# A two-layer transformer kernel: the normalised rows of the dense parts turned by way of DRAM and DVE instead of TensorE

## The chip, the cores and the metric

The kernel runs on one core of one Trainium2 chip. The metric is the device time of one execution in microseconds, as the median of several runs. Five engines are named as the profile names them: PE (TensorE, with its weight loads as PEld), DVE (VectorE), ACT (ScalarE), POOL (GpSimd) and SP (SyncE). Each has a queue of its own that it works off in order. Transfers are done by 16 DMA engines; in this kernel SP's queue issues them.

## The reference

A stack of attention, dense, attention, dense, over S = 2048 rows of D = 576 columns, with the same weights both times. The attention is linear, with 32 heads of 18 columns, the dense part has F = 4608 hidden features:

```python
x = A_x
x = x + _A_ref(_layernorm(x, axis=-1), A_wqkv, A_w_phi, A_wo)
x = x + _B_ref(_layernorm(x, axis=-1), B_w1, B_b1, B_w2, B_b2)
x = x + _A_ref(_layernorm(x, axis=-1), A_wqkv, A_w_phi, A_wo)
x = x + _B_ref(_layernorm(x, axis=-1), B_w1, B_b1, B_w2, B_b2)

def _B_ref(x, w1, b1, w2, b2):
    h = jnp.einsum("bsd,df->bsf", x, w1) + b1
    h = jnp.where(h > 0, h, 0) ** 2
    return jnp.einsum("bsf,fd->bsd", h, w2) + b2
```

`_A_ref` projects to queries, keys and values, applies a learned map and two softmaxes per head to queries and keys, forms the linear attention through the sums over all rows of key times value, and projects back. All sums over the rows' keys must be there before any row of that layer's attention can leave. `_layernorm` takes mean and variance of each row and has no weights.

## The kernel before, in words

**Tiles.** The rows are cut into 4 blocks of TB = 512, a block into NT = 4 tiles of P = 128. The 576 columns are KC = 4 chunks of 128 and one of DT = 64. Every operand of a matmul is split into a high part (rounded to the matmul's format) and a low part (what the rounding left), and three products stand for one. An operand must lie with the summed dimension on the partitions, so rows that were normalised must be turned: from 128 rows x 576 columns to columns x rows.

**The norm** (`Norm`, L329-397) works on one block. For tile t: `stats` (L351 and L360 on DVE, the reciprocal root on POOL), `scale` (L371, L372 on DVE: subtract the mean, multiply), `turn` (L386: four transposes of 128x128 on PE into PSUM; L387: the high part copied out by ACT; L388: the low part by DVE). For half h, which is two tiles, `rest` does the same with the last 64 columns (L395, L396, L397).

**The dense part** (`g_mlp`) runs per block over f = 0 to 35, each 128 hidden features. `hidden(f)` is 14 matmuls (L824), `square(f)` the bias, relu (L829, ACT), square (L830, ACT) and the split (L833 cast and L834 subtraction, DVE), `second(f - 1)` the way back, 12 matmuls by rows (L849) and 3 by features (L841). PE's order is hidden(f), second(f - 1), hidden(f + 1), and so on. The PSUM bank of `hidden` has one buffer from f = 2 on, so relu(f) must have read it before hidden(f + 1) starts. The weights come from DRAM by SP, one tile of 640 KB (`m_..h`, L787) and one of 576 KB (`m_..s`, L799) per f.

**What lies between.** `g_mlp` is a generator that yields after each hidden and each second. `weave` takes one slot of a plan at each yield, and the plan holds the attention's work, spread over the slots: `Plan.put(turn, depth, call)` puts a call into slot 2 x turn + 1, within a slot the greater depth first. The emitted order is each engine's order. A block of the dense part carries the attention of the next block (`plan_attend`), and in layer 0 also the keys and values of layer 1 for the block that was finished before it (`plan_keys`). Layer 0 works through blocks 3, 2, 0, 1, and layer 1 through 1, 0, 3, 2.

**The norms that the change touches.** `plan_norm` (L696) places one norm's steps. It is called in `plan_attend` (six norms: a_2, a_0, a_1 in layer 0 and a_0, a_3, a_2 in layer 1, in the last third of the dense block before) and in `plan_keys` (three norms, in the first iterations of a dense block: n_3 in m_2, n_2 in m_0, n_0 in m_1). The norms of the opening, of the passage between the layers and of the last keys are placed by other code and stay as they are. After `scale`, `out.keep` (L691) adds b2 to a row tile of the attend norms and stores it (L694); `g_mlp` loads it again at its end (L911). In `plan_keys`, `spill` writes the turned rows to DRAM for the second layer's queries.

In the profile m_2 is the dense part of block 2, a_0n.. the attend norm of block 0, n_2.. the keys norm of block 2, k_2.. the keys that follow it.

Of the kernel before, what the change touches and what calls it, by code (L numbers as in the profile page):

```python
# [21 lines left out]
def layers_kernel(  # L22
# [18 lines left out]
    nc = tc.nc  # L41
    S, D = x_in.shape[1], x_in.shape[2]
# [280 lines left out]
    def xt_tiles(name):  # L323
        return {"h": sb.tile([P, NC, TB], F32R, tag="xh", name=f"{name}h"),
                "l": sb.tile([P, KC, TB], F32R, tag="xl", name=f"{name}l")}

    class Norm:
# [62 lines left out]
        def rest(self, h):  # L390
# [5 lines left out]
            nc.scalar.activation(xh[:DT, KC, rows], pt[:DT, : TB // 2], AF.Copy)  # L396
            nc.vector.tensor_sub(xh[DT:, KC, rows], pt[:DT, : TB // 2], xh[:DT, KC, rows].bitcast(F32))  # L397
# [7 lines left out]
    def spill(b, x, parts=range(4)):  # L405
        for i in parts:
            d, piece = xt_part(b, x, i)
            nc.sync.dma_start(d, piece)
# [284 lines left out]
            nc.vector.tensor_add(x, x, b2t)  # L693
            nc.sync.dma_start(xm[self.b][t], x)  # L694

    def plan_norm(plan, norm, x_of, stats, scales, turns, rests, late=()):  # L696
        for t in range(NT):
            plan.put(stats[t], 0, lambda t=t: norm.stats(t, x_of(t)))
            plan.put(scales[t], 1, norm.scale, t)
            plan.put(turns[t], -1 if t in late else 2, norm.turn, t)  # L700
        for h in range(2):
            plan.put(rests[h], 2, norm.rest, h)

# [34 lines left out]
    def plan_attend(plan, at, gap, layer, b, raws, dst, name, o, queries=None):  # L738

        out = Out(layer, b, [], name)  # L740
        out.pair, calls = o
        if queries:
            for t in range(NT):
                plan.put(at + gap * t, 0, queries, t)
            at += 1
        for n, call in enumerate(calls):
            plan.put(at + n, 9, call)
        at = plan_queries(plan, at, gap, layer, raws, [], out.ph, name) + 1
        for i in range(2 * NG):
            plan.put(at + i / 2, 0, out.turn, i)  # L750
            plan.put(at + (i + 1) / 2, 1, out.times, i)
        at += NG + 1
        for t in range(NT):
            plan.put(at + t - 1, 9, out.load, t)
        plan_norm(plan, Norm(dst, f"{name}n", out.keep), out.project, [at + t for t in range(NT)],
                  [at + 1, at + 2, at + 4, at + 5], [at + 4 + t for t in range(NT)], [at + 5, at + 7])


    def g_mlp(layer, b, x, after, name, fresh, apart, final):
# [584 lines left out]
    def plan_keys(plan, prev_rows, last, keep):  # L1344
# [1 line left out]
        pb, done = prev_rows  # L1346
        m = f"1_{pb}"
        xk, es, ks, vts = {}, {}, {}, {}
        plan_norm(plan, Norm(xk, f"n{m}"), lambda t: done[t], (0, 0, 1, 2), (1, 1, 2, 3), (2, 3, 4, 4.5), (3, 5), (3,))
        (vw, vcalls), (kw, kcalls) = asked("v", f"w{m}"), asked("k", f"w{m}", TAGS_C)  # L1350
        for n in range(4):
            plan.put(8 + n if last else 2 + n / 2, 9, vcalls[n])
            plan.put(n / 2, 9, kcalls[n])
        if not last:
            for n in range(4):
                plan.put(5 + n / 2, -1, lambda n=n: spill(pb, xk, [n]))

        def keys(t):
            ks[t] = make_raw(xk, t, kw, f"k{m}k")
# [50 lines left out]
```

## Time and profile before

| | |
|---|---|
| median of 3 runs | 2529.17 us (2528.23 to 2530.25) |
| profiled execution, its own time | 2530.61 us |
| its span in the trace | 2528.9 us, 37324 instructions |
| granted TensorE clock | 1.00 in every stage |
| DMA packets of SP's queue | 161118, 503.10 MB |
| read from and written to DRAM | 418.39 and 84.64 MB, 199 GB/s over the span |

The span runs from the first to the last instruction of the trace; the run's own time has a little around it. A row of a timeline gives the start and the duration in microseconds, the engine, the line, the operation with its output and inputs, the shapes, how many equal neighbours are merged (x), and in brackets how long the engine stood idle before and what ended that. A row of the groups gives the count, the busy time in microseconds and the mean in ns, then the idle time ahead of the group. The layer's and the tile's number are left out of the names, so a_0np stands for all tiles of that kind in both layers.

### The profile page before, as it was taken

What the parts mean: (1) busy time and instruction counts of PE and PEld (TensorE: products, weight loads), DVE (VectorE), ACT (ScalarE), POOL (GpSimd) and SP (SyncE); (2) the same over time, 40 slices, a digit from 0 to 9 for tenths busy, and PEclk for the clock granted to TensorE, in tenths of its full rate; (3) what the DMA queues carried; (4) which work ended last, traced back from release to release, by engine and by line L of the source; (5) the groups of instructions that cost most, each with busy time, mean ns of one, the idle gap of its engine ahead of it and who ended that gap; (6) DMA issues with size and microseconds to landing.
All of it is one profiled execution on the core that took longest, in us unless ns stands there. A gap on an engine that the chain in (4) does not pass through costs nothing.

```text
span 2528.9 us, 37324 instructions
## 1 busy us (share of the span) xinstructions
PE 2512.7 (99%) x15300; PEld 2215.4 (88%) x15300; DVE 1166.8 (46%) x1986; ACT 741.9 (29%) x1268; POOL 113.4 (4%) x275
## 2 busy tenths in 40 slices
PE   9999999999999999999999999999999999999999
PEld 8998888888888988888888988888888888888887
DVE  6887955434634446345113775332353326332112
ACT  5544443322222222223223332222222222222221
POOL 4302000000000000000000010000000000000000
PEclk9999999999999999999999999999999999999999
DMA  9514887867647576484665345457544665456565
GB/s 318 174 53 138 288 280 259 309 216 265 214 148 261 179 262 213 147 272 147 196 198 168 115 142 189 152 192 258 183 161 155 221 231 164 148 187 230 195 193 174
DMA packets 161288, 505.48 MB, mean 200 GB/s; under 512 B 21350, under 2 KB 49798, under 8 KB 161118
## 3 DMA queue, kind: packets, MB, share of 16 engines
q1 hardware_dynamic: 161118, 503.10, 59.8%
q8 instruction: 121, 1.98, 0.3%
q14 instruction: 49, 0.40, 0.0%
HBM read 418.39 MB, written 84.64 MB: 199 GB/s over the span
## 4 chain that ended last, share of the span: by engine, by line
PE 97%; DMA 1%; DVE 1%; ACT 0%; issue 0%; SPq 0%; DVEq 0%; ACTq 0%
PE m_1ph L824 9%; PE m_3ph L824 9%; PE m_0ph L824 9%; PE m_2ph L824 9%; PE m_1acc L849 7%; PE m_3acc L849 7%; PE m_2acc L849 7%; PE m_0acc L849 7%; PE m_1acc L841 2%; PE m_3acc L841 2%; PE m_2acc L841 2%; PE m_0acc L841 2%; PE a_2po L686 1%; PE a_0po L686 1%; PE kvp L527 1%; PE a_3po L686 1%
## 5 line engine op out<-in xcount | busy, mean ns | idle before, releaser
L824 PE MATMUL m_2ph<-a_2nh,m_2h 128*128 128x512 f32 x720 | 225.4, 395 | 2.1 <-DMA m_2h<-dw 2.1
L824 PE MATMUL m_0ph<-a_0nh,m_0h 128*128 128x512 f32 x720 | 226.3, 396 | 0.2 <-DMA m_0h<-dw 0.2
L849 PE MATMUL m_3acc<-m_3s,m_3hb 128*128 128x448 f32 x864 | 189.7, 367 | 0.3 <-DVE m_3hb L833 0.3
L849 PE MATMUL m_0acc<-m_0s,m_0hb 128*128 128x448 f32 x864 | 189.9, 368 | 0.0
L849 PE MATMUL m_1acc<-m_1s,m_1hb 128*128 128x448 f32 x864 | 189.4, 367 | 0.3 <-PE m_1ph L824 0.3
L849 PE MATMUL m_2acc<-m_2s,m_2hb 128*128 128x448 f32 x864 | 189.6, 367 | 0.0
L849 PEld LDWEIGHTS m_1acc<-m_1s,m_1hb 128*128 128x128 f32 x864 | 161.5, 188 | 18.2 <-PE m_1ph L824 0.5
L833 DVE CAST m_2hb<-m_2hr 128x512 fp32r<-128x512 f32 x72 | 30.8, 427 | 317.8 <-ACT m_2hr L830 317.4
L849 PEld LDWEIGHTS m_3acc<-m_3s,m_3hb 128*128 128x128 f32 x864 | 161.2, 188 | 17.8 <-PE m_3ph L824 0.5
L849 PEld LDWEIGHTS m_2acc<-m_2s,m_2hb 128*128 128x128 f32 x864 | 160.7, 188 | 16.1
L849 PEld LDWEIGHTS m_0acc<-m_0s,m_0hb 128*128 128x128 f32 x864 | 160.3, 188 | 15.6
L824 PEld LDWEIGHTS m_2ph<-a_2nh,m_2h 128*128 128x128 f32 x720 | 135.3, 188 | 32.8 <-issue 2.5
L824 PEld LDWEIGHTS m_0ph<-a_0nh,m_0h 128*128 128x128 f32 x720 | 135.3, 188 | 30.5 <-issue 0.6
L833 DVE CAST m_1hb<-m_1hr 128x512 fp32r<-128x512 f32 x72 | 30.7, 427 | 269.2 <-ACT m_1hr L830 269.2
L829 ACT ACTIVATE m_2hr<-m_2ph,b1t 128x512 f32<-128x512 f32 x72 | 49.6, 689 | 353.7 <-PE m_2ph L824 353.7
L833 DVE CAST m_0hb<-m_0hr 128x512 fp32r<-128x512 f32 x72 | 30.8, 427 | 260.8 <-ACT m_0hr L830 255.2
L829 ACT ACTIVATE m_0hr<-m_0ph,b1t 128x512 f32<-128x512 f32 x72 | 49.6, 689 | 334.3 <-PE m_0ph L824 334.3
L829 ACT ACTIVATE m_1hr<-m_1ph,b1t 128x512 f32<-128x512 f32 x72 | 49.6, 689 | 323.2 <-PE m_1ph L824 323.2
L829 ACT ACTIVATE m_3hr<-m_3ph,b1t 128x512 f32<-128x512 f32 x72 | 49.6, 689 | 240.3 <-PE m_3ph L824 240.3
L824 PE MATMUL m_3ph<-t0onh,m_3h 128*128 128x512 f32 (+1 forms) x380 | 113.3, 385 | 0.7 <-ACT t0onh L387 0.5
L833 DVE CAST m_3hb<-m_3hr 128x512 fp32r<-128x512 f32 x72 | 30.7, 426 | 180.5 <-ACT m_3hr L830 180.5
L824 PE MATMUL m_1ph<-t1onh,m_1h 128*128 128x512 f32 (+1 forms) x380 | 113.2, 385 | 0.6 <-ACT t1onh L387 0.5
(1934 smaller groups left out, 5618.8 us busy)
## 6 DMA issues: line engine op xcount, KB each, us to landing
m_2h<-dw SPq DMA_DIRECT2D x72, 640.0 KB
m_0h<-dw SPq DMA_DIRECT2D x72, 640.0 KB
m_1h<-dw SPq DMA_DIRECT2D x72, 640.0 KB
m_2s<-dw SPq DMA_DIRECT2D x72, 576.0 KB
m_0s<-dw SPq DMA_DIRECT2D x72, 576.0 KB
m_1s<-dw SPq DMA_DIRECT2D x72, 576.0 KB
dw<-m_3h SPq DMA_DIRECT2D x36, 640.0 KB
m_3h<-dw SPq DMA_DIRECT2D x36, 640.0 KB
```

The source lines that it names most:

```text
L527: nc.tensor.matmul(po[32 * q : 32 * q + 32, :, j], vt[:, h * VW : h * VW + 32], e[:, :, h * DH : (h + 1) * DH], start=not stay, stop=True, ...
L686: nc.tensor.matmul(pt[:, :HP], a, m[:w, g], start=(g == 0 and k == 0), stop=(g == NG - 1 and k == 2))
L824: nc.tensor.matmul(ph[:, cols], a, m, start=(k == 0), stop=(k == 3 * KC + 1))
L829: nc.scalar.activation(hr, ph, AF.Relu, bias=b1t[:, f : f + 1])
L833: nc.vector.tensor_copy(hh, hr)
L841: nc.tensor.matmul(acc[KC], a, m, start=(f == 0 and k == 0), stop=(f == NF - 1 and k == 2))
L849: nc.tensor.matmul(acc[t][:, :R], a[:, rows], m, start=(f == 0 and k == 0), stop=(f == NF - 1 and k == 2))
```

## The change

A class `StoredNorm` takes the place of `Norm` in `plan_attend` and `plan_keys`. Its `scale` writes the scaled rows into a tile whose 4 x 4 blocks of 32 columns are exchanged. `store` (two transfers) writes them to DRAM in that order, `fetch` (one transfer, and for every odd tile another for the last 64 columns) reads them back with every fourth row in a partition group, so that after it the element (row, column) has to move within 32 x 32 only. `turn` and `rest` then use DVE's transpose of 32 x 32 blocks (L438, L449), ACT copies the high part (L441, L452), DVE subtracts for the low part (L442, L453); the reordering left is in the access patterns of these three. All these transfers are issued by ACT. `store` stands half a turn, which is one slot, after `scale`; `fetch` has a time of its own. Both have depth -1, so they come last in their slot. For the keys norms stats and scales move forward, turns and rests half a turn back, and the spill one turn back; for the attend norms two scales move forward by a turn, and turns and rests stay. The 9 norms have 20 transposes each on PE before, 180 in all, and none after; DVE gets 54 transposes, ACT's queue 126 transfers.

```diff
--- before.py
+++ after.py
@@ -68,6 +68,8 @@
 
     xs = [[dram.tile([P, D], F32, name=f"xs{b}_{t}") for t in range(NT)] for b in range(NB)]
     xm = [[dram.tile([P, D], F32, name=f"xm{b}_{t}") for t in range(NT)] for b in range(NB)]
+    xrm = [dram.tile([NT, KC, P, P], F32, name=f"xrm{b}") for b in range(NB)]
+    xrt = [dram.tile([NT, DT // 32, P, 32], F32, name=f"xrt{b}") for b in range(NB)]
     xth = [dram.tile([P, NC * TB], F32, name=f"xth{b}") for b in range(NB)]
     xtl = [dram.tile([P, KC * TB], F32, name=f"xtl{b}") for b in range(NB)]
     dense1 = [dram.tile([P, 2 * NC * P], F32, name=f"dw1_{f}") for f in range(NF)]
@@ -396,6 +398,60 @@
             nc.scalar.activation(xh[:DT, KC, rows], pt[:DT, : TB // 2], AF.Copy)
             nc.vector.tensor_sub(xh[DT:, KC, rows], pt[:DT, : TB // 2], xh[:DT, KC, rows].bitcast(F32))
 
+    class StoredNorm(Norm):
+
+        def __init__(self, dst, name, b, then=None):
+            super().__init__(dst, name, then)
+            self.b, self.row = b, {}
+
+        def scale(self, t):
+            x, (mv, rstd) = self.x.pop(t), self.stat.pop(t)
+            row = self.row[t] = sb.tile([P, D], F32, tag="qk", name=f"{self.name}r{t}", bufs=5)
+            args = dict(scalar1=mv[:, 0:1], scalar2=rstd, op0=ALU.subtract, op1=ALU.mult)
+            nc.vector.tensor_scalar(row[:, : KC * P].rearrange("p (a b c) -> p b a c", a=KC, b=KC),
+                                    x[:, : KC * P].rearrange("p (b a c) -> p b a c", a=KC, b=KC), **args)
+            nc.vector.tensor_scalar(row[:, KC * P :], x[:, KC * P :], **args)
+            if self.then:
+                self.then(t, x)
+
+        def store(self, t):
+            row = self.row.pop(t)
+            nc.scalar.dma_start(xrm[self.b][t].rearrange("a p f -> p a f"),
+                                row[:, : KC * P].rearrange("p (a f) -> p a f", a=KC))
+            nc.scalar.dma_start(xrt[self.b][t].rearrange("a p f -> p a f"),
+                                row[:, KC * P :].rearrange("p (a f) -> p a f", f=32))
+
+        def fetch(self, t):
+            xn = self.xn[t] = sb.tile([P, KC * P], F32, tag="xn", name=f"{self.name}n{t}")
+            nc.scalar.dma_start(xn, xrm[self.b][t].rearrange("a (r g) f -> (a r) (g f)", g=KC))
+            if t % 2:
+                if self.xd is None:
+                    self.xd = sb.tile([P, TB // 2], F32, tag="xd", name=f"{self.name}e", bufs=1)
+                nc.scalar.dma_start(self.xd[t // 2 * DT : (t // 2 + 1) * DT].rearrange("p (t f) -> p t f", t=2),
+                                    xrt[self.b][t - 1 : t + 1].rearrange("t a (r g) f -> (a r) t (g f)", g=KC))
+
+        def turn(self, t):
+            xn, dst = self.xn.pop(t), self.dst
+            if t == 0:
+                dst.update(xt_tiles(self.name))
+            rows = slice(t * P, (t + 1) * P)
+            nc.vector.transpose(xn, xn)
+            src = xn.rearrange("p (g b r) -> p b g r", g=KC, b=KC)
+            hi, lo = (z[:, :KC, rows].rearrange("p b (r g) -> p b g r", g=KC) for z in (dst["h"], dst["l"]))
+            nc.scalar.activation(hi, src, AF.Copy)
+            nc.vector.tensor_sub(lo, src, hi.bitcast(F32))
+
+        def rest(self, h):
+            xh = self.dst["h"]
+            rows = slice(h * TB // 2, (h + 1) * TB // 2)
+            own, far = (slice(i * DT, (i + 1) * DT) for i in (h, 1 - h))
+            xd = self.xd[own]
+            nc.vector.transpose(xd, xd)
+            src = xd.rearrange("p (t g r) -> p t g r", t=2, g=KC)
+            hi, lo = (xh[z, KC, rows].rearrange("p (t r g) -> p t g r", t=2, g=KC) for z in (own, far))
+            nc.scalar.activation(hi, src, AF.Copy)
+            nc.vector.tensor_sub(lo, src, hi.bitcast(F32))
+
     XT = (("h", xth, 0, KC // 2), ("l", xtl, 0, KC // 2), ("h", xth, KC // 2, NC), ("l", xtl, KC // 2, KC))
 
     def xt_part(b, x, i):
@@ -693,11 +749,13 @@
             nc.vector.tensor_add(x, x, b2t)
             nc.sync.dma_start(xm[self.b][t], x)
 
-    def plan_norm(plan, norm, x_of, stats, scales, turns, rests, late=()):
+    def plan_norm(plan, norm, x_of, stats, scales, fetches, turns, rests):
         for t in range(NT):
             plan.put(stats[t], 0, lambda t=t: norm.stats(t, x_of(t)))
             plan.put(scales[t], 1, norm.scale, t)
-            plan.put(turns[t], -1 if t in late else 2, norm.turn, t)
+            plan.put(scales[t] + 0.5, -1, norm.store, t)
+            plan.put(fetches[t], -1, norm.fetch, t)
+            plan.put(turns[t], 2, norm.turn, t)
         for h in range(2):
             plan.put(rests[h], 2, norm.rest, h)
 
@@ -752,8 +810,9 @@
         at += NG + 1
         for t in range(NT):
             plan.put(at + t - 1, 9, out.load, t)
-        plan_norm(plan, Norm(dst, f"{name}n", out.keep), out.project, [at + t for t in range(NT)],
-                  [at + 1, at + 2, at + 4, at + 5], [at + 4 + t for t in range(NT)], [at + 5, at + 7])
+        plan_norm(plan, StoredNorm(dst, f"{name}n", b, out.keep), out.project, [at + t for t in range(NT)],
+                  [at + 1, at + 2, at + 3, at + 4], [at + 2.5, at + 3.5, at + 4.5, at + 5.5],
+                  [at + 4 + t for t in range(NT)], [at + 5, at + 7])
 
 
     def g_mlp(layer, b, x, after, name, fresh, apart, final):
@@ -1346,14 +1405,15 @@
         pb, done = prev_rows
         m = f"1_{pb}"
         xk, es, ks, vts = {}, {}, {}, {}
-        plan_norm(plan, Norm(xk, f"n{m}"), lambda t: done[t], (0, 0, 1, 2), (1, 1, 2, 3), (2, 3, 4, 4.5), (3, 5), (3,))
+        plan_norm(plan, StoredNorm(xk, f"n{m}", pb), lambda t: done[t], (0, 0, 0.5, 1), (0.5, 0.5, 1, 1.5),
+                  (1.5, 1.5, 3, 3.5), (2.5, 3, 4.5, 5), (3.5, 5.5))
         (vw, vcalls), (kw, kcalls) = asked("v", f"w{m}"), asked("k", f"w{m}", TAGS_C)
         for n in range(4):
             plan.put(8 + n if last else 2 + n / 2, 9, vcalls[n])
             plan.put(n / 2, 9, kcalls[n])
         if not last:
             for n in range(4):
-                plan.put(5 + n / 2, -1, lambda n=n: spill(pb, xk, [n]))
+                plan.put(6 + n / 2, -1, lambda n=n: spill(pb, xk, [n]))
 
         def keys(t):
             ks[t] = make_raw(xk, t, kw, f"k{m}k")
```

The lines of the changed kernel after L397 are shifted; where L824 and L849 stood, its rows have L883 and L908.

PE near the end of block m_2, in the iteration of hidden features 33 and 32, before. The names: a_0np is the PSUM tile of the transposes, a_0nn the scaled rows, a_0ne their last 64 columns.

```order
L824 MATMUL m_2ph_8303<-a_2nl,m_2h_33_8247 128x512
L824 MATMUL m_2ph_8303<-a_2nh,m_2h_33_8247 128x512 x3
L386 MATMUL a_0np_8324<-ident,a_0nn_8101 128x128 [waits DVE_49]
L386 MATMUL a_0np_8324<-ident,a_0nn_8101 128x128 x3
L395 MATMUL a_0np_8331<-ident,a_0ne 64x128 [waits DVE_49]
L395 MATMUL a_0np_8331<-ident,a_0ne 64x128
L849 MATMUL m_2acc_5928<-m_2s_32_8245,m_2hb_8267 128x448 [waits DMAHW0_49]
```

The same place on PE in the changed kernel:

```order
L883 MATMUL m_2ph_8323<-a_2nl,m_2h_33_8267 128x512
L883 MATMUL m_2ph_8323<-a_2nh,m_2h_33_8267 128x512 x3
L908 MATMUL m_2acc_5934<-m_2s_32_8259,m_2hb_8287 128x448 [waits DMAHW5_49,DVE_49]
L908 MATMUL m_2acc_5934<-m_2s_32_8259,m_2hb_8287 128x448
L908 MATMUL m_2acc_5934<-m_2s_32_8259,m_2hb_8287 128x448 [waits DVE_49]
L908 MATMUL m_2acc_5935<-m_2s_32_8259,m_2hb_8287 128x448 x3
```

The six transposes between hidden(33) and second(32) are gone, and nothing stands in their place.

ACT in the first iterations of block m_0 in layer 0, which carries the keys norm n_2, before: relu and square of f = 1, 2 and 3, and the copy of the first turned tile between them.

```order
L829 ACTIVATE m_0hr_8539<-m_0ph_8524,b1t 128x512 [waits PE_49]
L830 ACTIVATE m_0hr_8539<-m_0hr_8539 128x512 [waits Activation_49]
L829 ACTIVATE m_0hr_8624<-m_0ph_8609,b1t 128x512 [waits DVE_49,PE_49]
L830 ACTIVATE m_0hr_8624<-m_0hr_8624 128x512 [waits Activation_49]
L387 ACTIVATE n_2h<-n_2p_8653 128x4x128 [waits PE_49]
L829 ACTIVATE m_0hr_8688<-m_0ph_8673,b1t 128x512 [waits DVE_49,PE_49]
```

The same stretch of ACT in the changed kernel, from the store of tile 1 (n_2r_8594) to relu of f = 3. xrm and xrt are the new DRAM tensors, n_2r the rows that are stored, n_2n and n_2e what comes back; DMAHW0 to DMAHW7 are the eight semaphores that all transfers of the kernel share in turn.

```order
L419 DMA xrm_103<-n_2r_8594 128x4x128 [waits DMAHW4_49,DVE_49]
L421 DMA xrt_107<-n_2r_8594 128x2x32 [waits DMAHW6_49,DVE_49]
L888 ACTIVATE m_0hr_8640<-m_0ph_8625,b1t 128x512 [waits PE_49]
L889 ACTIVATE m_0hr_8640<-m_0hr_8640 128x512 [waits Activation_49]
L426 DMA n_2n_8650<-xrm_103 128x512 [waits DMAHW7_49,DMAHW0_49]
L426 DMA n_2n_8652<-xrm_103 128x512 [waits DMAHW4_49,DMAHW1_49]
L430 DMA n_2e<-xrt_107 64x2x128 [waits DMAHW6_49,DMAHW3_49,DMAHW2_49]
L419 DMA xrm_103<-n_2r_8608 128x4x128 [waits DVE_49]
L421 DMA xrt_107<-n_2r_8608 128x2x32 [waits DVE_49]
L419 DMA xrm_103<-n_2r_8647 128x4x128 [waits DMAHW7_49,DVE_49]
L421 DMA xrt_107<-n_2r_8647 128x2x32 [waits DMAHW1_49,DVE_49]
L888 ACTIVATE m_0hr_8697<-m_0ph_8682,b1t 128x512 [waits PE_49]
```

Between relu 2 and relu 3 ACT now issues seven transfers. Fetch 0 and fetch 1 wait for the landing of the stores of tiles 0 and 1, and the store of tile 3 (n_2r_8647) waits for the semaphores DMAHW7 and DMAHW1, which fetch 0 and fetch 1 took.

DVE in the same block, from the split of f = 2 on, before: the low part of a turned tile, then the next tile's scale and statistics, then the split of f = 3.

```order
L833 CAST m_0hb_8627<-m_0hr_8624 128x512 [waits PE_49,Activation_49]
L834 TENSOR_TENSOR m_0hb_8627<-m_0hr_8624,m_0hb_8627 128x512 [waits DVE_49]
L388 TENSOR_TENSOR n_2l<-n_2p_8653,n_2h 128x4x128 [waits Activation_49]
L371 TENSOR_SCALAR n_2n_8660<-m_2x_8462,n_2m_8602,n_2d_8603 128x512 [waits Pool_49]
L372 TENSOR_SCALAR n_2e<-m_2x_8462,n_2m_8602,n_2d_8603 128x64
L833 CAST m_0hb_8691<-m_0hr_8688 128x512 [waits Activation_49]
```

DVE in the changed kernel, from the split of f = 3 to rest 0, behind the split of f = 4:

```order
L892 CAST m_0hb_8700<-m_0hr_8697 128x512 [waits PE_49,Activation_49]
L893 TENSOR_TENSOR m_0hb_8700<-m_0hr_8697,m_0hb_8700 128x512 [waits DVE_49]
L438 STREAM_TRANSPOSE n_2n_8650<-n_2n_8650 128x512 [waits DMAHW7_49]
L442 TENSOR_TENSOR n_2l<-n_2n_8650,n_2h 128x4x4x32 [waits Activation_49]
L438 STREAM_TRANSPOSE n_2n_8652<-n_2n_8652 128x512 [waits DMAHW1_49]
L442 TENSOR_TENSOR n_2l<-n_2n_8652,n_2h 128x4x4x32 [waits Activation_49]
L892 CAST m_0hb_8754<-m_0hr_8751 128x512 [waits PE_49,Activation_49]
L893 TENSOR_TENSOR m_0hb_8754<-m_0hr_8751,m_0hb_8754 128x512 [waits DVE_49]
L449 STREAM_TRANSPOSE n_2e<-n_2e 64x256 [waits DMAHW3_49]
L453 TENSOR_TENSOR n_2h<-n_2e,n_2h 64x2x4x32 [waits Activation_49]
```

Two transposes of DVE, each with the subtraction that waits for ACT's copy, stand between the splits of f = 3 and f = 4, and rest 0 behind the latter; the first keys matmul of block n_2 needs both.

## The prediction

> **What bounds the kernel now.** I read the page's engine line first, then its chain that ended last, then PE's timeline where the changed norms stand, and last ACT, DVE and SP there.
>
> ```profile
> span 2528.9 us, 37324 instructions
> PE 2512.7 (99%) x15300; PEld 2215.4 (88%) x15300; DVE 1166.8 (46%) x1986; ACT 741.9 (29%) x1268; POOL 113.4 (4%) x275
> PE 97%; DMA 1%; DVE 1%; ACT 0%; issue 0%; SPq 0%; DVEq 0%; ACTq 0%
> q1 hardware_dynamic: 161118, 503.10, 59.8%
> ```
>
> PE is busy for 2512.7 of 2528.9 us and carries 97% of the chain. DVE works for 46% and ACT for 29% of the span, the DMA engines for 59.8%. So time is saved only by taking work from PE, and lost only where another engine or a transfer keeps PE waiting. What a transpose costs PE is read from the distance between equal matmuls, not from its duration:
>
> ```profile
> L386 PE MATMUL a_0np<-ident,a_0nn 128*128 128x128 f32 x32 | 4.8, 272 | 0.0
> ```
>
> The 32 transposes of this group last 272 ns each, yet the group is busy for only 4.8 us, 0.15 us each, because matmuls overlap. The first timeline is block m_2's, with the attend norm a_0 (the norm whose rows feed the next block); in the second, of block m_0 with the keys norm n_2 (whose rows feed the next layer's keys), the first interval has no transpose:
>
> ```profile
> 775.04 0.40 PE L824 MATMUL m_2ph<-a_2nh,m_2h 128*128 128x512 f32 x1
> ...
> 778.26 0.60 PE L386 MATMUL a_0np<-ident,a_0nn 128*128 128x128 f32 x4
> 778.61 2.69 PE L849 MATMUL m_2acc<-m_2s,m_2hb 128*128 128x448 f32 x12
> ...
> 781.84 0.39 PE L824 MATMUL m_2ph<-a_2nh,m_2h 128*128 128x512 f32 x1
> ...
> 785.09 0.60 PE L386 MATMUL a_0np<-ident,a_0nn 128*128 128x128 f32 x4
> 785.53 0.38 PE L395 MATMUL a_0np<-ident,a_0ne 128*64 128x128 f32 x2
> 785.67 2.68 PE L849 MATMUL m_2acc<-m_2s,m_2hb 128*128 128x448 f32 x12
> ...
> 788.86 0.40 PE L824 MATMUL m_2ph<-a_2nh,m_2h 128*128 128x512 f32 x1
> ```
>
> ```profile
> 812.80 2.63 PE L849 MATMUL m_0acc<-m_0s,m_0hb 128*128 128x448 f32 x12
> ...
> 819.17 2.60 PE L849 MATMUL m_0acc<-m_0s,m_0hb 128*128 128x448 f32 x12
> ...
> 822.30 0.60 PE L386 MATMUL n_2p<-ident,n_2n 128*128 128x128 f32 x4
> 822.65 0.48 PE L824 MATMUL m_0ph<-a_0nh,m_0h 128*128 128x512 f32 x1
> ...
> 826.00 2.60 PE L849 MATMUL m_0acc<-m_0s,m_0hb 128*128 128x448 f32 x12
> ...
> 832.98 2.60 PE L849 MATMUL m_0acc<-m_0s,m_0hb 128*128 128x448 f32 x12
> ```
>
> A plain iteration takes 819.17 - 812.80 = 6.37 us. With a turn (four transposes) it takes 781.84 - 775.04 = 6.80 in m_2 and 826.00 - 819.17 = 6.83 in m_0; with a turn and a rest (two more) 788.86 - 781.84 = 7.02 and 832.98 - 826.00 = 6.98. None of these rows shows idle time ahead: PE never waits for the norms.
>
> **The part that goes.** A turn costs 0.43 to 0.46 us, a rest on top of it 0.15 to 0.22. The attend norm pays 2 x 0.43 + 2 x 0.65 = 2.16 us, the keys norm 4 x 0.46 + 2 x 0.15 = 2.14. Nine norms (six in attend, three in keys) pay 9 x 2.15 = **19.4 us** for 180 transposes, 0.11 us each. The lower bound comes from the starts: the matmul behind a turn starts 778.61 - 778.26 = 0.35 us after it, behind turn and rest 785.67 - 785.09 = 0.58, so 2 x 0.35 + 2 x 0.58 = 1.86 per norm, 16.7 in all. I take the periods, since they also hold the slower start of the matmuls behind (2.69 us against 2.60).
>
> [...]
>
> **What is added on DVE.** 54 transposes that the trace doesn't show. Per element the nearest rows are the scale, which also reads and writes SBUF, and the slowest form per element, the reciprocal:
>
> ```profile
> L371 DVE TENSOR_SCALAR a_0nn<-a_0x,a_0nm,a_0nd 128x512 f32<-128x512 f32 x8 | 4.3, 543 | 0.0
> L388 DVE TENSOR_TENSOR n_2l<-n_2p,n_2h 128x512 fp32r<-128x512 f32 x8 | 5.5, 688 | 7.2 <-ACT n_2h L387 7.2
> L491 DVE RECIPROCAL a_2r<-a_2r 128x64 f32<-128x64 f32 x8 | 4.4, 554 | 0.3
> L727 DVE RECIPROCAL a_2u<-a_2u 128x32 f32<-128x32 f32 x8 | 2.8, 353 | 0.3
> ```
>
> A transpose of 128x512 lies between 0.54 us, the scale's, and 3.3 us by the reciprocal: 32 more elements cost it 554 - 353 = 201 ns, 6.3 ns each, 512 of them 3.2, and 0.15 fixed. I take 0.55, the scale's: it too streams a row from SBUF to SBUF at one read, while a reciprocal is arithmetic of many steps. At 0.55 the 36 long and 18 short ones (0.28) are 25 us on an engine that idles for 1362 us. Splitting into high and low parts stays, on ACT and DVE, from SBUF instead of PSUM; from rows of these engines I see no reason for another price than 0.6 and 0.7.
>
> At the end of a block the turn of tile 3 and rest 1 lie behind the last subtraction:
>
> ```profile
> 800.97 0.69 DVE L834 TENSOR_TENSOR m_2hb<-m_2hr,m_2hb 128x512 fp32r<-128x512 f32 x1
> ...
> 802.29 0.42 DVE L397 TENSOR_TENSOR a_0nh<-a_0np,a_0nh 64x256 fp32r<-64x256 f32 x1
> ```
>
> ```profile
> 806.31 0.40 PE L824 MATMUL m_0ph<-a_0nh,m_0h 128*128 128x512 f32 x1
> ```
>
> From 801.66: transpose 0.55, copy 0.58, subtraction 0.69, short transpose 0.28, copy 0.37, subtraction 0.42, together 2.9, so done at 804.6. The next block's first matmul starts at 806.31 - 0.66 = 805.65 when its iteration is shorter. Cover 1.1 us, price nothing.
>
> **What is added on ACT and the queues.** ACT issues 14 transfers per norm (two stores per tile, four fetches, two of the last columns), 126 in all; 0.29 MB out and back per tile, 36 x 0.59 = 21 MB, 4% of the traffic. The trace has no transfer on ACT's queue; SP's rows price issue and landing:
>
> ```profile
> 395.33 0.45 SPq L770 DMA_DIRECT2D m_3rr<-in_B_w  x1
> 395.81 1.22 SPq L162 DMA_DIRECT2D m_3rr<-in_B_w  x2
> ...
> 751.42 0.32 SPq L694 DMA_DIRECT2D xm<-a_0x  x1
> 753.51 0.32 SPq L911 DMA_DIRECT2D m_2x<-xm  x1
> ```
>
> An issue takes 0.32 us, 0.45 for 512 runs of 512 bytes as the new store has, and 0.61 each (1.22 for two) right behind such a one. A load of rows waits until their 288 KB store has landed: 753.51 - 751.42 = 2.09 us, my value for a landing. The far bound is a 640 KB load amid other traffic:
>
> ```profile
> 498.30 3.59 SPq L787 DMA_DIRECT2D m_2h<-dw  x2
> ```
>
> ```profile
> 506.71 0.47 PE L824 MATMUL m_2ph<-a_2nh,m_2h 128*128 128x512 f32 x1 [2.06 <-DMA m_2h<-dw]
> ```
>
> 8.4 us from issue to use. In attend norms store and fetch lie a whole iteration apart (6.37 us or more), so ACT's wait at the fetch is over before it begins: nothing. The keys norms are tight. ACT's rows there:
>
> ```profile
> 819.37 0.69 ACT L829 ACTIVATE m_0hr<-m_0ph,b1t 128x512 f32<-128x512 f32 x1 [5.02 <-PE m_0ph L824]
> ...
> 826.21 0.69 ACT L829 ACTIVATE m_0hr<-m_0ph,b1t 128x512 f32<-128x512 f32 x1 [2.67 <-PE m_0ph L824]
> ```
>
> ```profile
> 818.98 0.31 DVE L372 TENSOR_SCALAR n_2e<-m_2x,n_2m,n_2d 128x64 f32<-128x64 f32 x1
> ```
>
> The hidden bank of PSUM is single: relu (L829) must be done before the next hidden matmuls start. ACT's new order there is relu 2, fetches 0 and 1, stores 2 and 3, relu 3. Fetch 1 waits for the landing of store 1, and store 3 for the landings of fetches 0 and 1, whose semaphores it shares. Behind them stands relu 3. Without the turn its matmuls end at 826.00 - 0.46 = 825.5, the next hidden ones start 3.1 us later (822.30 - 819.17, the work between) at 828.6, and relu 3 must start by 827.9. Store 1 can be issued at 819.29; with its issue 0.45, the fetch's 0.32 and store 3's two 0.45 and 0.32, the two landings may take 827.9 - 819.29 - 1.54 = **7.1 us** together. Two of 2.09 leave 2.9 us spare. The issues also push relu 2 from 819.37 by 0.6 us (quiet) to about 2.5 (busy), and it is needed by 822.30 - 0.69 = 821.6: none or 0.3 late. Before the first keys matmul the chain relu 4, square, cast, subtraction, rest 0 ends about 0.7 us ahead of its use. So 0 (all fits) to about 2 us per norm; below nothing the waits cannot go. I take 0.7, **2.1 us** in all.
>
> SP's queue is reordered only in block m_2, where the fetch of the last key weights moves; the 2.06 us wait above may vanish, or come again behind the moved spill of the turned rows. I count neither; it is the lower end.
>
> **Sum.** -19.4 + 2.1 = -17.3 us. The profiled execution took 2530.61 us, 1.7 more than its span and 1.44 more than the median of the runs; 2530.61 - 17.3 = 2513.3, less 1.4: **2512**. With no stall and without the 2.06 us it is 2507.5, with 16.7 saved and 2 us per norm 2518.5.
>
> **Rivals.** *Half eaten (0.18).* Landings of 5 us in the keys blocks, between 2.09 and 8.4: 10 - 7.1 = 2.9 us late at relu 3, about 3.3 with rest 0, three times: 10 us back, 2520. For it: the DMA engines are 59.8% busy and weights of 640 and 576 KB are under way. Against: 2.09 us was measured in the same kind of stage.
>
> *Slower (0.09).* ACT's queue blocks: both landings take 8.4 us, relu 3 is 16.8 - 7.1 = 9.7 us late, three times 29 us against 19.4: 2539. It decides from landings of (7.1 + 19.4 / 3) / 2 = 6.8 us on. Against: that row's load is twice as large and stood behind another. [...] No row here shows two queues at once.
>
> *Same (0.06).* Transposes of 3.3 us: in the keys blocks two of them with copy and subtraction hold DVE for 2 x 4.6 = 9.2 us between sub 3 and cast 4, rest 0 comes about 5 us late, three times 15, and the block ends lose about 1: 2512 - 2.1 to 2526 after -19.4 + 16. For it only that the instruction is not in the trace.
>
> *The change does not do what it says (0.01).* The order of PE's instructions shows the transposes gone, so only if their slots were filled by waits of another kind: 2529.
>
> **How the numbers follow.** My forecast has 0.60, which with the half-eaten case makes 0.78; 0.06 is left for what I haven't thought of, split evenly over the signs and toward faster. The range 2507 to 2521 holds both cases. About 0.2% (5 us) is what a measurement of this kernel can tell from no change: faster 0.60 + 0.18 + 0.04 = 0.82, same 0.06 + 0.01 + 0.02 = 0.09, slower 0.09.
>
> **What would show it.** PE's iterations with a turn at 6.37 us, PE's busy time near 2493, DVE's transposes near 0.55 us, and ACT's relu 3 in m_0 within 2.4 us of its matmuls' end. PE rows with idle time behind ACT's relu in the keys blocks show the second and third case by their length; DVE transposes over 2 us the fourth. Idle time in attend norms, or iterations still near 6.8 us, would make the prediction wrong at its root.

## The result and the profile after

The changed kernel takes 2544.09 us (median of 4 runs, 2542.14 to 2550.82) against 2529.71 before: ratio 1.0062, 95% interval 1.0042 to 1.0081. It is slower by 14.4 us; 2512 was forecast. First the page of the changed kernel, engines, chain and the two DMA queues (q1 is SP's, q10 is ACT's):

```profile
span 2542.8 us, 37215 instructions
PE 2505.4 (99%) x15120; PEld 2204.5 (87%) x15120; DVE 1214.1 (48%) x2040; ACT 766.1 (30%) x1268; POOL 114.0 (4%) x275
PE 93%; DMA 3%; DVE 2%; ACT 2%; issue 0%; ACTq 0%; POOL 0%; SPq 0%; DVEq 0%
...
q1 hardware_dynamic: 161118, 503.10, 59.1%
q10 hardware_dynamic: 36576, 21.24, 2.9%
```

The 180 transposes are gone (15300 to 15120), yet PE's busy time fell by 7.3 us only, and its idle time rose from 16.2 (2528.9 - 2512.7) to 37.4 us (2542.8 - 2505.4). The chain now runs for 7% of the span through DMA, DVE and ACT. Where the norm has no wait, the gain is there: in block m_2, with the four turns of a_0, features (three matmuls, L900) follow each other in the time of plain iterations, 6.42 and 6.35 us:

```profile
787.38 0.86 PE L900 MATMUL m_2acc<-m_2hb,m_2s 128*128 128x512 f32 x3
...
793.80 0.86 PE L900 MATMUL m_2acc<-m_2hb,m_2s 128*128 128x512 f32 x3
...
800.15 0.86 PE L900 MATMUL m_2acc<-m_2hb,m_2s 128*128 128x512 f32 x3
```

What PE waits for: in all, how often and the longest, all of it in layer 0 (the waits at the kernel's start and those under 1 us are left out):

```profile
PE m_0ph L883 <- ACT m_0hr L888: 6.5, 2, 3.6
PE m_3ph L883 <- ACT m_3hr L888: 4.7, 2, 4.1
PE m_2ph L883 <- DMA m_2h<-dw: 3.2, 2, 2.1
PE k_0kp L483 <- DVE n_0h L453: 2.2, 1, 2.2
PE m_2py L989 <- ACT m_2yt L967: 2.2, 1, 2.2
PE m_0py L989 <- ACT m_0yt L967: 2.2, 1, 2.2
PE m_1ph L883 <- ACT m_1hr L888: 1.9, 1, 1.9
...
PE k_3kp L483 <- DVE n_3h L453: 1.1, 1, 1.1
```

Three kinds: the hidden matmuls wait for relu (6.5 + 4.7 + 1.9 = 13.1 us), the transposes of `yt` at a block's end for ACT's copy (4.4), the keys for rest 0 (3.3). The wait for m_2h is 1.1 longer than before. The first kind read on ACT's queue, block m_0 with the keys norm n_2, from store 0 to relu 3:

```profile
826.62 0.38 ACTq L419 DMA_DIRECT2D xrm<-n_2r  x1
...
827.76 0.48 ACTq L419 DMA_DIRECT2D xrm<-n_2r  x1
...
829.09 0.69 ACT L888 ACTIVATE m_0hr<-m_0ph,b1t 128x512 f32<-128x512 f32 x1 [6.20 <-DMA xrm<-n_2r]
...
831.56 3.62 ACTq L426 DMA_DIRECT2D n_2n<-xrm  x2
...
839.85 0.37 ACTq L421 DMA_DIRECT2D xrt<-n_2r  x1
840.26 0.69 ACT L888 ACTIVATE m_0hr<-m_0ph,b1t 128x512 f32<-128x512 f32 x1 [9.82 <-DMA xrm<-n_2r]
```

Fetch 0 can start 4.9 us after store 0. The two fetches are merged in one row of 3.62 us; an issue lasts 0.34, so fetch 1 starts at 831.56 + 3.62 - 0.34 = 834.84, 7.1 us after store 1. The last transfer waits for fetch 1 and starts 5.0 us after it. Behind these stands relu 3, 840.26. PE at that place:

```profile
841.01 0.79 PE L883 MATMUL m_0ph<-a_0nh,m_0h 128*128 128x512 f32 x1 [3.57 <-ACT m_0hr L888]
841.60 0.63 PE L883 MATMUL m_0ph<-a_0nl,m_0h 128*128 128x512 f32 x1
...
846.99 2.61 PE L908 MATMUL m_0acc<-m_0s,m_0hb 128*128 128x448 f32 x12
```

After 3.57 us without work the 14 hidden matmuls take 846.99 - 841.01 = 5.98 us, where in the kernel before they took 815.97 to 819.17 = 3.2 us undisturbed; a matmul lasts 0.63 us instead of 0.39. An attend norm of layer 0 shows the same on ACT at the end of m_0, where relu stands behind the fetch of the last columns, 1117.95 - 1106.95 = 11.0 us after their store:

```profile
1106.95 0.46 ACTq L421 DMA_DIRECT2D xrt<-a_1nr  x1
...
1117.95 0.59 ACTq L430 DMA_DIRECT2D a_1ne<-xrt  x1
```

The stretches of the changed kernel say what slows the matmuls, in their last three columns (granted clock, DMA share, GB/s):

```profile
826.00:835.00 9.00, 9.00 (x43) 7.67 (x42) 6.06 (x16) 1.32 (x2) 3.37 (x15) 1.00 0.97 316
841.01:846.99 5.98, 5.98 (x15) 4.67 (x15) 3.46 (x5) 2.35 (x3) 0.00 (x0) 0.52 0.55 187
1960.00:2005.00 45.00, 45.00 (x230) 39.58 (x229) 21.34 (x42) 11.83 (x16) 2.37 (x6) 1.00 0.77 242
```

Behind the wait the granted clock is 0.52. The DMA engines are busy for 97% of the time while the stores and fetches above are under way (first row); the last row is an attend norm of layer 1, where PE waits for nothing, at 77%. Its landings are not short for that: fetch 3 starts there 7.7 us after store 3 (1999.53 - 1991.88), and relu is in time all the same. The kernel before, its first row around the store and load that gave 2.09 us, its second the keys stage of m_0:

```profile
750.00:770.00 20.00, 20.00 (x114) 18.10 (x114) 7.71 (x20) 2.64 (x4) 1.58 (x4) 1.00 0.53 169
810.00:835.00 25.00, 25.00 (x120) 21.45 (x119) 13.40 (x32) 7.85 (x13) 3.68 (x16) 1.00 0.80 250
```

The operations that took PE's place, in groups of the changed kernel:

```profile
L441 ACT ACTIVATE a_0nh<-a_0nn 128x512 fp32r<-128x512 f32 x8 | 9.0, 1122 | 15.8 <-DVE a_0nn L438 15.8
L442 DVE TENSOR_TENSOR a_0nl<-a_0nn,a_0nh 128x512 fp32r<-128x512 f32 x8 | 8.7, 1088 | 10.5 <-ACT a_0nh L441 10.5
L438 DVE STREAM_TRANSPOSE a_0nn<-a_0nn 128x512 f32<-128x512 f32 x8 | 5.6, 705 | 0.0
```

The transpose takes 0.70 us, the copy 1.12 instead of 0.60, the subtraction 1.09 instead of 0.69. At the end of block m_2 they stand on ACT ahead of the copy of `yt`, the second view being PE's:

```profile
807.49 1.11 ACT L441 ACTIVATE a_0nh<-a_0nn 128x512 fp32r<-128x512 f32 x1 [1.84 <-DVE a_0nn L438]
810.23 0.65 ACT L452 ACTIVATE a_0nh<-a_0ne 64x256 fp32r<-64x256 f32 x1 [1.62 <-DVE a_0ne L449]
810.90 0.60 ACT L967 ACTIVATE m_2yt<-m_2acc 128x512 f32<-128x512 f32 x1
```

```profile
811.55 0.66 PE L989 MATMUL m_2py<-ident,m_2yt 128*128 128x128 f32 x4 [2.21 <-ACT m_2yt L967]
```

**The account.** 19.4 us were to go from PE's work. In the run without DRAM below the same 180 transposes take 2512.7 - 2495.6 = 17.1 us with them; here the busy time fell by 7.3, so 9.8 us came back. Nearly all of it is matmuls at the lower clock: 2.8 behind the wait above, about 1.7 behind each of four other waits (2.09 us for m_2h, 2.21 at the block end, 2.93 and 4.12 for relu), 9.4 in all. Idle time adds 37.4 - 16.2 = 21.2. Together -17.1 + 9.8 + 21.2 = 13.9, the difference of the spans.

### The profile page after: what moved, and what is told of

Its sections match the earlier page's. It is cut to its first block, busy times and chain, and to the rows that moved or that the text cites. A ratio compares the mean times of both kernels' runs of the same rounds, so it can differ in the third digit from the quotient of the medians.

```text
span 2542.8 us, 37215 instructions
## 1 busy us (share of the span) xinstructions
PE 2505.4 (99%) x15120; PEld 2204.5 (87%) x15120; DVE 1214.1 (48%) x2040; ACT 766.1 (30%) x1268; POOL 114.0 (4%) x275
## 4 chain that ended last, share of the span: by engine, by line
PE 93%; DMA 3%; DVE 2%; ACT 2%; issue 0%; ACTq 0%; POOL 0%; SPq 0%; DVEq 0%
PE m_0ph L883 9%; PE m_3ph L883 9%; PE m_2ph L883 9%; PE m_1ph L883 9%; PE m_1acc L908 7%; PE m_3acc L908 7%; PE m_2acc L908 6%; PE m_0acc L908 6%; PE m_1acc L900 2%; PE m_3acc L900 2%; PE m_2acc L900 2%; PE m_0acc L900 2%; PE a_2po L742 1%; PE a_0po L742 1%; PE kvp L583 1%; PE a_3po L742 1%
## 5 line engine op out<-in xcount | busy, mean ns | idle before, releaser
L883 PE MATMUL m_0ph<-a_0nh,m_0h 128*128 128x512 f32 x720 | 229.9, 401 | 6.5 <-ACT m_0hr L888 6.5
L883 PE MATMUL m_2ph<-a_2nh,m_2h 128*128 128x512 f32 x720 | 226.5, 396 | 3.2 <-DMA m_2h<-dw 3.2
L908 PE MATMUL m_3acc<-m_3s,m_3hb 128*128 128x448 f32 x864 | 189.6, 367 | 0.3 <-DVE m_3hb L892 0.3
L908 PE MATMUL m_1acc<-m_1s,m_1hb 128*128 128x448 f32 x864 | 189.4, 367 | 0.4 <-PE m_1ph L883 0.4
L908 PE MATMUL m_2acc<-m_2s,m_2hb 128*128 128x448 f32 x864 | 189.7, 368 | 0.0
L908 PE MATMUL m_0acc<-m_0s,m_0hb 128*128 128x448 f32 x864 | 189.5, 367 | 0.0
L908 PEld LDWEIGHTS m_1acc<-m_1s,m_1hb 128*128 128x128 f32 x864 | 161.6, 188 | 18.4 <-PE m_1ph L883 0.5
L908 PEld LDWEIGHTS m_3acc<-m_3s,m_3hb 128*128 128x128 f32 x864 | 161.2, 188 | 17.8 <-PE m_3ph L883 0.5
L908 PEld LDWEIGHTS m_2acc<-m_2s,m_2hb 128*128 128x128 f32 x864 | 161.3, 188 | 16.4
L908 PEld LDWEIGHTS m_0acc<-m_0s,m_0hb 128*128 128x128 f32 x864 | 160.7, 188 | 16.0
L883 PEld LDWEIGHTS m_0ph<-a_0nh,m_0h 128*128 128x128 f32 x720 | 138.0, 192 | 38.5 <-ACT m_0hr L888 7.4
L883 PEld LDWEIGHTS m_2ph<-a_2nh,m_2h 128*128 128x128 f32 x720 | 136.1, 189 | 34.7 <-issue 2.5
L883 PE MATMUL m_3ph<-t0onh,m_3h 128*128 128x512 f32 (+1 forms) x380 | 114.3, 388 | 5.3 <-ACT m_3hr L888 4.7
L883 PE MATMUL m_0ph<-a_0nl,m_0h 128*128 128x512 f32 x288 | 115.0, 399 | 0.0
L883 PE MATMUL m_1ph<-a_1nh,m_1h 128*128 128x512 f32 x360 | 112.5, 394 | 1.9 <-ACT m_1hr L888 1.9
```

The lines of the kernel that those rows point to most:

```text
L883: nc.tensor.matmul(ph[:, cols], a, m, start=(k == 0), stop=(k == 3 * KC + 1))
L908: nc.tensor.matmul(acc[t][:, :R], a[:, rows], m, start=(f == 0 and k == 0), stop=(f == NF - 1 and k == 2))
```

## The experiments

Theory Q: ACT works its queue in order and stands at transfers that land late because the weights fill the DMA engines; relu behind them keeps PE waiting, and the clock falls. Rivals: B, the 21 MB slow the weights themselves; W, the longer copies, subtractions and hand-offs between DVE and ACT are the cause; R, the short runs of the stores make the landings long. Each ratio is against runs of the kernel before that were made along with it (medians 2529.35 to 2530.18 us), and differences between runs are taken by way of these.

**POOL issues all transfers.**

```diff
-            nc.scalar.dma_start(...)   # all four, in store and fetch
+            nc.gpsimd.dma_start(...)
```

> The changed kernel with its 126 transfers issued by POOL instead of ACT; the plan stays. Theory Q (queue): the transfers land 5 to 11 us after their issue, ACT stands at them, and the relu behind them keeps PE waiting; PE then runs some us at a lower clock. By Q the waits of PE for relu in the keys blocks (3.57 + 2.78 lower clock, 1.85), in m_0's last iterations (2.93 + 1.7) and in m_3 (4.7 + 1.65) go, those for yt at the block ends and for rest 0 stay: 2544 - 19 = about 2525. Theory B (bandwidth): the 21 MB more delay the weights themselves: no change, 2544. Theory W (work): the longer copies and subtractions of the turn (1.1 us instead of 0.6 and 0.7) and their hand-offs between DVE and ACT are what makes relu late: no change, 2544.

Measured: 2549.07 us, ratio 1.0078 (1.0064 to 1.0092). The waits for relu went as Q says: 0 in m_0 and m_1, 1.3 left in m_3. The time did not. PE's waits in this kernel:

```profile
PE k_2kp L483 <- DVE n_2h L453: 4.1, 1, 4.1
PE k_3kp L483 <- ACT n_3h L441: 3.6, 1, 3.6
PE k_3kp L483 <- DVE n_3h L453: 3.0, 1, 3.0
PE k_0kp L483 <- DVE n_0h L453: 3.0, 1, 3.0
```

Now the keys wait for their rows. In m_0 the first store leaves POOL at 833.23, after the statistics of tiles 2 and 3, which stand ahead of it on POOL; scale 0 was done at 827.11, 6.1 us before. PE's waits for that block's turned rows are 4.1, 1.8 and 0.6 us, about as much. So relu's waits were what Q says, but POOL's own order held the store back by 6.1 us, and whether the rows would be in time if it left at once, this run does not show.

**SP issues all transfers** (the same edit with `nc.sync`).

> The changed kernel with its transfers issued by SP. What stands behind a wait pays: relu's waits go, and the loads of the weights, which SP issues, stand behind the waits for the stores' landings. Theory Q: PE waits for m_..h and m_..s instead, as long or longer than for relu, 2545 to 2560. If the weights are loaded far enough ahead to hide it, 2530.

Measured: 2548.05 us, ratio 1.0072 (1.0058 to 1.0085), as Q expects. Its waits:

```profile
PE m_2ph L883 <- DMA m_2h<-dw: 9.3, 4, 4.7
PE m_0ph L883 <- DMA m_0h<-dw: 6.9, 2, 3.5
PE m_1ph L883 <- DMA m_1h<-dw: 3.0, 1, 3.0
```

Relu's waits are gone but for 1.2 us in m_3, and the weights, which SP issues behind its own waits, come late by more. With ACT it is relu that pays, with SP the weights: what stands behind the waits on the engine that issues. This kernel also has a keys stage with less traffic, as the weights are held back; SP's queue and, below it, the DMA share:

```profile
829.12 0.44 SPq L419 DMA_DIRECT2D xrm<-n_2r  x1
...
833.14 0.45 SPq L426 DMA_DIRECT2D n_2n<-xrm  x1
```

```profile
828.00:834.00 6.00, 6.00 (x29) 5.12 (x29) 4.66 (x14) 1.32 (x2) 2.10 (x5) 1.00 0.69 185
```

Fetch 1 starts 4.0 us after store 1 at a share of 0.69; it was 7.1 at 0.97, and 2.09 at 0.53 before the change. A high share alone doesn't make a landing long, though: the changed kernel's store at 1082.85 had landed 2.6 us later, by its semaphore, at a share of 0.97 in that time. The bytes already under way fit better. Of the 36 stores of 256 KB in the changed kernel's trace, the 6 that found at most 0.7 MB of other transfers issued and not yet landed took 2.3 to 4.9 us to land, the 4 that found over 2 MB took 7.8 to 10.0 (from the records of issues and semaphores).

**Turned by DVE without DRAM.**

```diff
+    class LocalNorm(Norm):   # turn and rest of StoredNorm, on the rows where they lie
-        plan_norm(plan, Norm(...)
+        plan_norm(plan, LocalNorm(...)
```

> The kernel before, with the nine norms turned by DVE's transpose, ACT's strided copy and DVE's subtraction in the old slots, but without any store or fetch (each 32x32 block is turned where it lies, so the rows are not turned as a whole: part of the computation is left out). Q and B: 19.4 us go from PE, the block ends still pay for the copies ahead of yt (2 x 2.2 and 1.65 at a lower clock): 2529.7 - 19.4 + 6 = about 2516. W: the stalls stay, 2535 or more.

Measured: 2518.45 us, ratio 0.9959 (0.9944 to 0.9974). All of DVE's and ACT's new work with none of the transfers is 11 us faster than before: the loss needs the transfers, and W alone is out. What W has left is 2.2 us of wait at each of the two block ends and 2.2 in m_3.

**Transfers without their use.**

```diff
+    class MirrorNorm(Norm):   # scales once more into a row tile, stores it, fetches into a spare tile
-        plan_norm(plan, Norm(...)
+        plan_norm(plan, MirrorNorm(...)   # stores and fetches on ACT
```

> The kernel before, turned on PE as ever, with the stores and fetches of the nine norms added on ACT's queue at like slots (a second scale on DVE fills the stored tile, and nothing reads what is fetched). Q and B: stalls of relu as in the changed kernel, about 15 us: 2545. W: only the 0.9 us of DVE per tile, hidden: 2530 to 2532.

Measured: 2539.67 us, ratio 1.0041 (1.0028 to 1.0055). Ten of the expected 15 us: PE waits for relu in the three keys blocks (2.1, 2.0 and 0.6 us) and for a turned tile (1.3), and is busy 4.2 us longer for the same matmuls. The attend norms wait for nothing here, as two of four stores and fetches stand later and nothing uses the rows. The last two runs together would give -10.9 + 10.3 = -0.6 us, not 14.4. So about 15 us come only in the change itself, where the turn depends on the fetch and the norms' steps stand at other places; the waits that the change has and neither of these runs has are most of relu's in the attend norms (4.7 us in m_3, 2.93 in m_0) and the keys' for rest 0 (3.3), with the lower clock behind them.

**The attend norms alone, and the keys norms alone.**

```diff
-        plan_norm(plan, StoredNorm(xk, f"n{m}", pb), ...)      # attend alone: the keys norms as before
+        plan_norm_pe(plan, Norm(xk, f"n{m}"), ...)             # plan_norm_pe is plan_norm of before
```

> The change for the six attend norms alone, with ACT issuing; the three keys norms are turned on PE as before. From the trace of the changed kernel: 13 us go from PE, and PE's waits in the last third of layer 0's blocks stay (m_3 4.7 + 1.65 at the lower clock, m_0 2.93 + 1.7, the two block ends 4.4 + 1.65): 2529.4 - 13 + 17 = 2533. The rest of the 14 us is then the keys norms'. If every stored norm cost alike (theory W), six of nine would lose two thirds: 2539.

> The change for the three keys norms alone, with ACT issuing; the six attend norms are turned on PE as before. The attend norms alone cost 2.8 us against the kernel before, all nine 14.5. If the two kinds don't touch each other, the keys norms alone cost the rest, about 12: 2541. If the attend norms' transfers make the keys norms' waits worse (the nine together cost more than the parts), less: 2535.

Measured: 2532.30 us, ratio 1.0011 (1.0002 to 1.0020), and 2540.16 us, ratio 1.0041 (1.0025 to 1.0056). The parts, 2.8 and 10.0 us, make 12.8 of the 14.4, within the change's own interval (10.6 to 20.5 us): that the kinds touch each other is not shown. Three keys norms of nine carry most of the loss. ACT's rows with the keys norms alone:

```profile
821.30 0.47 ACTq L419 DMA_DIRECT2D xrm<-n_2r  x1
...
827.76 0.34 ACTq L426 DMA_DIRECT2D n_2n<-xrm  x1
...
833.41 0.37 ACTq L421 DMA_DIRECT2D xrt<-n_2r  x1
```

6.5 us from store 1 to fetch 1, 5.7 from fetch 1 to the last transfer: the landings are as long without the attend norms' share.

**The attend norms alone, issued by POOL.**

```diff
-            nc.scalar.dma_start(...)   # on the kernel with the attend norms alone
+            nc.gpsimd.dma_start(...)
```

> As the kernel with the attend norms alone, but POOL issues their transfers. Theory Q (ACT stands at transfers, relu is behind it): relu's waits go, as they did with POOL issuing all nine; the block ends (2.1 + 1.6 + 1.7) and 1.3 in m_3 stay: 2529.4 - 13 + 6.7 = 2523. Theory W: POOL changes nothing against ACT.

Measured: 2523.93 us, ratio 0.9982 (0.9972 to 0.9991). Nothing but the issuer differs from 2532.30: 8.4 us were ACT standing at transfers and the clock that fell behind it (PE's busy time makes 2507.4 - 2501.5 = 5.9 of the 10.1 us between the two traces). What is left are the block ends (2.2 and 1.5 us), 1.4 us for m_2h and 1.3 for relu in m_3.

**The last turn half a turn earlier.**

```diff
-                  [at + 4 + t for t in range(NT)], [at + 5, at + 7])
+                  [at + 4, at + 5, at + 6, at + 6.5], [at + 5, at + 6.5])
```

> As the kernel with the attend norms alone and POOL issuing, with the last turn and rest 1 half a turn earlier, so that ACT's copies come ahead of relu 35 instead of between it and the copy of yt. If the waits at the block ends come from these copies standing ahead of yt on ACT, they go: 2523 - 5 + 0.7 = about 2519. If they come from something else in the last iteration, 2523.

Measured: 2526.86 us, ratio 0.9990 (0.9982 to 0.9999): 3 us slower, not 4 faster. The waits for `yt` went as expected; PE's rows show what came:

```profile
803.13 1.47 PE L908 MATMUL m_2acc<-m_2hb,m_2s 128*128 128x512 f32 x3 [2.68 <-DVE m_2hb L900]
...
1114.95 1.65 PE L908 MATMUL m_0acc<-m_0hb,m_0s 128*128 128x512 f32 x3 [2.68 <-DVE m_0hb L900]
```

Now the split of f = 35 stands behind the turn, later by 2.68 us, and the matmuls after it are slow (1.47 and 1.65 us for three). The trace is one of the slower of 11 runs (2528.95 us in 2524.72 to 2529.57); its mean granted clock is 0.999, and that of the 11 is 0.998 or 0.999. The chain of five hand-offs found no hole here either.

**Plain rows instead of every fourth column.**

```diff
-            src = xn.rearrange("p (g b r) -> p b g r", g=KC, b=KC)
+            src = xn.rearrange("p (b n) -> p b n", b=KC)   # and hi, lo likewise; rest the same
```

> The changed kernel with the copies and subtractions of turn and rest on plain rows of 128 instead of every fourth column (the columns come out in another order, so the turned rows are not in place: that part of the computation is changed). Measures what the strided access patterns cost: the copy should fall from 1.11 to about 0.6 us and the subtraction from 1.1 to 0.7. Theory Q: only the chains at the block ends, in m_3 and before the keys get shorter, the waits for landings stay: about 2538. Theory W: most of the loss goes, 2525 or less.

Measured: 2537.10 us, ratio 1.0027 (1.0016 to 1.0037). The copy takes 0.63 us, the subtraction 0.69: the strided patterns cost 0.5 and 0.4 us each time and 7 us of the 14 in all. Q's 2538 was near. So with the transfers there, the longer operations are worth half of the loss; without them (2518.45) they cost no more than the waits named there.

**Stores in long runs.**

```diff
-            nc.scalar.dma_start(xrm[self.b][t].rearrange("a p f -> p a f"), ...)
+            nc.scalar.dma_start(xrm[self.b][t].rearrange("a (r g) f -> (a r) (g f)", g=KC), row[:, : KC * P])   # xrt likewise
```

> The changed kernel with its stores written as one run of 2 KB (and of 256 bytes) per partition instead of 512 runs of 512 bytes and 256 of 128 (the rows come back in another order, so that part of the computation is changed); bytes, waits and places are the same. If the weights ahead of them in the DMA engines make the landings last 5 to 11 us (theory Q), nothing changes: 2544. If the short runs do (rival R), landings fall towards 2 us and the waits for relu go: 2530 or less.

Measured: 2540.01 us, ratio 1.0039 (1.0025 to 1.0053). R gets 4 to 5 us; in m_0 fetch 1 still starts 6.3 us after store 1 (7.1 with the short runs), and the waits for relu are still there (4.7 in m_3, 2.64 in m_0, 1.26 in m_1). The short runs are a part, not the cause. For the rest stand the shares and the bytes under way, shown above. No run changed the weights' traffic and nothing else, so that the weights make the landings long is argued from these rows and not isolated.

**Layer 1's attend norms alone.**

```diff
+        if layer:   # StoredNorm, ACT issues; else, and for the keys norms, Norm as before
```

> The change for the three attend norms of layer 1 alone; the three of layer 0 and the keys norms are turned on PE as before. In the trace of the changed kernel the three blocks of layer 1 show no wait of PE and gain about 2.2 us each. Q: 2529.7 - 6.5 = 2523. W: their chains are as long as elsewhere, so about 9/9 x 3 of the loss: slower than before, 2534.

Measured: 2523.54 us, ratio 0.9979 (0.9971 to 0.9988): three norms bring 5.8 us, 1.9 each or 0.10 per transpose, with no wait added on PE. The idea pays where its transfers are covered.

**A version that beats both.**

```diff
+    class HalfNorm(StoredNorm):   # tiles 0, 1 and rest 0 by DRAM; tiles 2, 3 and rest 1 by PE
+        if layer: StoredNorm      # all transfers issued by POOL; keys norms as before
+        else: HalfNorm
```

> A version to beat both: in layer 1 the change for the three attend norms; in layer 0 only tiles 0 and 1 and rest 0 of the three attend norms go by DRAM, tiles 2 and 3 and rest 1 are turned on PE as before, so that no copy of theirs stands ahead of yt; POOL issues all of these transfers; the keys norms stay on PE. 9.7 us go from PE (3 x 2.16 + 3 x 1.08), about 0.7 comes back in m_3: 2529.5 - 9 = 2520.5. If the copies of the first half already hold back relu, 2523 or more.

Measured: 2519.34 us, ratio 0.9958 (0.9946 to 0.9971): 10.8 us faster than before, 25 faster than the change. PE has no wait over 0.5 us left in layer 0's dense blocks, not even the 2.06 us for m_2h; the other 8.7 us are 0.10 for each of 90 transposes.

## Why the prediction was wrong

- **The part that goes** held: 0.11 us per transpose forecast, 0.10 measured where nothing waits (5.8 us for 60, 8.7 for 90), and 17.1 us instead of 19.4 for all 180.
- **The landing** is the step that failed: "2.09 us, my value for a landing", with "the far bound" of 8.4 us. Measured 4.9 to 7.1 us in m_0's keys stage. The 2.09 stood in a stage with a DMA share of 0.53; the keys stage had 0.80 before the change and, while the transfers are under way, 0.97 with it. The prediction had 59.8%, an average over the span, on the side of the rival and set it aside because 2.09 us "was measured in the same kind of stage", which the shares refute. From store 1 to relu 3 it had left 827.9 - 819.29 = 8.6 us; they took 840.26 - 827.76 = 12.5, so relu 3 was 3.9 us late, and PE waited 3.57. (Its 7.1 us for two landings had most of the issues taken off a second time, since a landing counted like the 2.09 holds one already.)
- **The attend norms**, "nothing": wrong in layer 0. In m_3 relu waited behind fetch 2, which started 10.1 us after its store (421.55 - 411.45), in m_0 behind the fetch of the last columns, 11.0 us after theirs; an iteration does not cover that, and both are over the far bound of 8.4. The change of issuer alone is worth 8.4 us. In layer 1 it was right: PE waited for nothing. Idle time in attend norms was the prediction's own sign of being wrong at its root.
- **The block end** was costed on the wrong reader. The chain was compared with the next block's first matmul (1.1 us of cover); the copy of `yt`, which stands behind it on ACT and which PE needs first, was overlooked, and copy and subtraction were taken at 0.6 and 0.7 us where every fourth column costs 1.1. That is 2.2 us twice.
- **The lower clock** was in no term: 9.4 us, two thirds of the whole loss. A wait was priced at its length.
- **The rivals**: "Slower" named the mechanism and gave 6.8 us as the landing from which it decides. Two landings of 6.0 on average fell below that and it was slower all the same, for the terms left out. "Same" (slow transposes) is out, 0.70 us. The stall of 2.06 us did not vanish (2.09).

## What to carry to other kernels

Price a new transfer by what is already under way in the stage where it will stand (a store of 256 KB took 2.3 to 4.9 us to land with at most 0.7 MB ahead of it, 7.8 to 10.0 with over 2 MB), not by the share of the span, and list everything that is queued behind its wait on the engine that issues it. A wait on the engine that bounds costs more than its length if the clock falls behind it: 3.57 us in m_0, and 2.8 more for the matmuls at 0.52. A norm moved off PE gains only where its transfers land before the work behind them is due; the same edit was worth 1.9 us per norm in layer 1 and cost 3.3 per keys norm in layer 0.

## What the runs showed of the hardware

- Gaps of PE of 2.09, 2.21, 2.93, 3.57 and 4.12 us were followed by matmuls at 0.63 instead of 0.39 us for 3.4 us each, and for 5.8 after that of 3.57; gaps of 0.57, 1.05, 1.12, 1.85, 2.20 and 2.25 us, and the 2.06 us before the change, were not. So near 2 us it isn't the length alone that decides in these two traces. In the changed kernel's the granted clock is 0.50 in five stretches, from 430.36, 512.28, 812.66, 839.96 and 1119.86 us on, and 1.00 between them; four last 3.41 us, the one from 839.96 on 6.83, and the starts lie 24, 88, 8 and 82 times 3.413 us apart. With the whole span cut into steps of that length, counted from these starts, the step ahead of each has 2.09 to 2.88 us of idle PE, any other 1.61 or less. The 2.21 us at the end of m_2 lie within one step, and the clock is at 0.50 in the next; the 2.20 us at the end of m_0 are cut by a step's edge into 0.61 and 1.59, and it stays at 1.00 (rows of the changed kernel, the first number behind the length being PE's busy time, and the clock the third from the end):

```profile
809.25:812.66 3.41, 1.20 (x9) 1.07 (x8) 2.63 (x6) 1.25 (x2) 0.00 (x0) 1.00 0.33 128
812.66:816.08 3.42, 3.42 (x10) 2.81 (x9) 1.97 (x7) 0.00 (x0) 0.00 (x0) 0.50 0.69 263
1126.68:1130.10 3.42, 2.81 (x13) 2.08 (x12) 2.22 (x4) 1.11 (x1) 0.00 (x0) 1.00 0.63 213
1130.10:1133.51 3.41, 1.82 (x11) 1.74 (x12) 2.67 (x8) 1.25 (x2) 0.00 (x0) 1.00 0.09 38
1133.51:1136.92 3.41, 3.41 (x17) 2.79 (x16) 1.19 (x3) 0.06 (x1) 0.00 (x0) 1.00 0.91 335
```

  The 2.06 us for m_2h before the change, cut into 1.44 and 0.62 by steps counted from 2526.79, where that trace's clock falls at the kernel's end, cost no clock: it is 1.00 on both sides. What sets the clock, these runs do not show.
- A copy on ACT with every fourth element written takes 1.12 us for 128x512, with plain rows 0.63; the subtraction on DVE 1.09 and 0.69. DVE's 32x32 transpose of 128x512 takes 0.70 us.
- POOL takes 0.55 to 1.01 us for each of these issues (all nine norms on POOL), ACT 0.34 to 1.03 with one of 2.89 (the changed kernel).
